# One Fourier filter and expert kernel: loads, small vector steps and one output bank moved in the order of work

## The chip, the cores and the metric

The kernel runs on one core of a Trainium2 chip. The metric is device time in microseconds (us) from launch to end. The engines of the core run side by side, each in the order of its own instruction stream: TensorE (PE, matrix products into PSUM; PEld its weight loads), VectorE (DVE), ScalarE (ACT), GpSimd (POOL, here the indirect scatters) and SyncE (SP, which issues most DMA transfers).

## The reference, cut to what matters

Each of 8 sequences of 2496 rows and 256 columns is filtered in the frequency domain; each filtered row then goes through the one of 8 experts that its gate prefers.

```python
X = np.fft.rfft(x, axis=1)
y = np.fft.irfft(X * (filt_r + 1j * filt_i), n=2496, axis=1)   # 8 x 2496 x 256
x = y.reshape(8 * 2496, 256)
logits = x @ w_gate                                            # 256 x 8
expert_idx = np.argmax(logits, axis=1)
gate_w = softmax(logits)[rows, expert_idx]
for e in range(8):
    h = np.maximum(x[expert_idx == e] @ w1[e], 0)              # 256 x 1024
    out[expert_idx == e] = gate_w * (h @ w2[e])                # 1024 x 256
```

## The kernel before

**Stages.** First the transform: 16 half sequences (8 sequences by 2 halves of the columns) go through a two-step Fourier transform, the filter and the way back. For a group t of four frequencies, `spec1` transposes (pt, copied to z), `spec2` multiplies (px), `filt_` and `join` apply the filter on VectorE (tr, ti, then p), and `spec3` goes back (pi, copied by ScalarE to U). `forward1` and `loadx` bring in the next half sequence. For each finished sequence `route1` to `route6` find expert and place of every row (plw, copied to lw, transposed to pgl, copied by VectorE to gl), and `inv1` to `inv3` finish its rows (pg, gt, py, yt) and scatter them with POOL into the DRAM buffer xs, sorted by expert. In the same stage the experts' weights are read (`w_load`), scaled by powers of two and stored as high and low f16 halves (wscr).

Then the experts: the sorted rows are worked in blocks of 128. There are 7 pairs of blocks ready after sequence 6, 63 pairs after the last sequence, and single blocks at the end. A pair or a single is a unit k. For a unit, `load` (line 1045) fetches the rows xb, 4 buffers; `loadw` (1077) fetches the first-layer weights wa and the second-layer weights wb of its expert, into one of two or four slots, and the transfer is skipped where the slot holds that expert already. Slots reuse the buffers named cm, bm, T and ff, so a weight load may bear these names, and a first-layer load goes to wa, cm or T, a second-layer load to wb, bm or ff. `prep` (1095 to 1104, VectorE) finds a row scale s, `split` scales the block to two f16 halves xs (1109 ScalarE, 1110 VectorE), `turn` (1124) has SP issue a transposing load xs to xt, one for each block of a pair. `layer1` (1146, into ph) has 24 products of 256 columns for two of a pair's four chunks; ScalarE applies the ReLU (hs, 1154) and the cast (hh, 1156), VectorE takes the difference (hl, 1162, `halves`). `layer2` (1177, into po) runs one unit later, in two parts i = 0 and 1 of 12 products each; then VectorE forms the gate factor g (1187), `out_` (1197) scales po with it, and `send` scatters the output.

**What sets the order.** Every step is entered in a list with `at(key, ...)`, the list is sorted by its key (a due time), and the engines' streams are written in that order. No engine passes over a waiting instruction. Keys of the expert stage count from the unit's due time z with its length u: in before, rows are loaded at z - 2.1 u, wa at about z - 1.24 u (or after the last user of the slot), the first block is prepared at z - 1.35 u, split 0.1 and turned 0.15 later.

**Banks.** The outputs po of all blocks share the one bank of the pool pO (tag pO, 1 buffer), the chunks ph the two of pH. The transform's tiles share pF (4 buffers), and plw, pgl and the other routing tiles the single bank of pD.

Of the kernel before, what the change touches and what calls it, by code (L numbers as in the profile page):

```python
# [9 lines left out]
F32 = mybir.dt.float32  # L10
# [5 lines left out]
ALU = mybir.AluOpType  # L16
# [5 lines left out]
S, D, E, F = 2496, 256, 8, 1024  # L22
# [123 lines left out]
def tile_fft_moe(ctx, tc, x, filt_r, filt_i, w_gate, w1, w2, cst, out):  # L146
    nc = tc.nc
    B = x.shape[0]
# [58 lines left out]
    with ExitStack() as fctx:  # L207
# [635 lines left out]
        ps = pD.tile([128, 512], F32, name="pwarm", tag="pD")  # L843
# [31 lines left out]
        def at(key, f, *a):  # L875
            work.append((key, f, a))
# [21 lines left out]
        RT = (0.0, 0.4, 0.65, 1.05, 1.5, 1.75, 2.5, 2.55, 2.9, 3.3)  # L898
        slow = lambda t: min(1.0, max(0.6, 1.0 - 0.06 * (t - 72)))
        for t in range(NT):  # L900
            u, it = divmod(t, 5)
            rho = slow(t)
            at(t, spec1, t)
            w = t + (0.98 if t % 2 == 0 and 3 < t < 72 else 0.0)
# [4 lines left out]
            if u + 1 < NU_ALL and it == 0:  # L909
                for j in range(6):  # L910
                    z = 4.02 + 0.1 * j if u < 1 else t + K["f"] + K["fd"] * j
                    at(z + 1.2 - 0.1 * j if u == 1 else z, forward1, u + 1, j)
            if u % 2 == 0 and it == 0 and u + 2 < NU_ALL:
                for c in range(5):
                    z = t + K["f"] + K["fd"] * (c if c < 4 else 5) + 0.35
# [5 lines left out]
        OPEN = 76.6  # L921
        done = []
        y2 = {}
        for b in range(B):
            rho = slow(10 * b + 9)
            s0 = 10 * b + 9 + K["s3"] * rho + 0.05
            c = 1.0 if b < B - 1 else 0.6
            v = 1.5 if b < B - 2 else c
            y = (0.5, 1.3, 2.1) if b < B - 2 else (0.4 * c, 0.9 * c, 1.2 * c)
            for i, f in enumerate(  # L930
                (
                    (route1, 0),
                    (route1b, 0),
                    (route1, 1),
                    (route1b, 1),
                    (route2,),
                    (route3,),
                    (route4,),
                    (route4b,),
                    (route5,),  # L940
                    (route6,),
                )
            ):
                at(s0 + v * RT[i], f[0], b, *f[1:])
            lead = 3.2 if b < B - 2 else 2.0 if b < B - 1 else 1.3


            t = 10 * b + 20
            d = 0.35
            if b < B - 1:  # L950
                z = PLACE[0] + 0.3 if b == B - 2 else t + K["s3"] * slow(t) - 0.15
                d = min(0.75, (z - s0 - lead) / (NPAIR - 1))
            for j in range(NPAIR):
                z = s0 + lead + (j // 2 * 2 if b < B - 2 else j) * d + 0.001 * j
                at(z, inv1, b, j)
                at(z + y[1], inv2, b, j)
                y2[b, j] = z + y[1]
                z = max(z + y[2], s0 + v * RT[9] + 0.1 + 0.9 * d * j)
                at(z, inv3, b, j)
            if b in [r for r, _, _ in SEG]:  # L960
                for s, part in enumerate(SEG):
                    if part[0] == b:
                        z0 = s0 + v * RT[9] + 0.2
                        for i in range(5):
                            at((96.0 + i) if s == 2 else z0 + (0.1, 0.25)[s] * i, finish, s)
            done.append(z)
# [4 lines left out]
        for q in range(2 * E):  # L971
            e, i = divmod(q, 2)
            z = K["w"] + K["wp"] * q
            at(z - 2.25, w_load, e, i)
            for d, f, *a in (
                (-0.1, w_max, 0),
                (0.1, w_max, 1),
                (0.15, w_turn),
                (2.3, w_scale),
                (2.37, w_hi, 0),  # L980
                (3.7, w_lo, 0),
                (4.37, w_hi, 1),
                (5.6, w_lo, 1),
                (5.7, w_out),
            ):
                at(z + d, f, e, i, *a)
# [5 lines left out]
        wa, wb, mps = [], [], []  # L992
        st = {}
        hid = {}
# [170 lines left out]
        def layer2(b, i):  # L1165
            k, j = home[b]
            m = units[k][2]
            w = wb[slot[k]]
            if i == 0:
                st[b] = (mps[2].tile([128, D], F32, name=f"po{b}", tag="pO"), *st[b][1:])  # L1170
            ps = st[b][0]
            wv = w[:, 0:4096].rearrange("p (i f d) -> p i f d", i=2, d=D)
            for f in range(4 * i, 4 * i + 4):
                c, e = divmod(f, 4 // m)
                o = (e * m + j) * 128
                for n, (q, r) in enumerate(((0, 0), (0, 1), (1, 0))):
                    nc.tensor.matmul(  # L1177
                        ps,
                        lhsT=hid[k, c][q][:, o : o + 128],
                        rhs=wv[:, r, f],  # L1180
                        start=(f == 0 and n == 0),
                        stop=(f == 7 and n == 2),
                    )
            if i:
                g0 = st[b][1]
                g = mps[0].tile([128, 1], F32, name=f"g{b}", tag="g", bufs=3)
                nc.vector.tensor_tensor(g, g0, w[:, 4096:4098].bitcast(F32), op=ALU.mult)
                st[b] = (ps, g, st[b][2])

        def out_(b):  # L1190
            ps, g, t = st.pop(b)
# [45 lines left out]
        for k in range(nu):  # L1237
            s, i, m, b0 = units[k]
            z, d, _ = tau[b0]
            u = d * m  # L1240
            at(max(opened(s), z - (2.1 * u if m > 1 else 2.0), OPEN + 0.1), load, k)
            old = [j for j in range(k) if slot[j] == slot[k]]
            for n in range(2):
                ahead = (
                    12 - 4 * i - 2 * n if s == 2 and i < 2 else 3.3 + 0.3 * k - 0.5 * n if k < 2 else 1.3 - 0.8 * n
                )
                t = when(old[-1], n) + 0.01 if old else 0.0
                at(max(opened(s) + 0.02, t, span(k)[0] - ahead, OPEN + 0.05), loadw, k, n)
            for q in range(m):
                y = max(opened(s) + 0.3, z - (2.1 if b0 < 2 else 1.35 * u if m > 1 else 1.4)) + 0.4 * d * q  # L1250
                at(y, prep, b0 + q)
                at(y + 0.1, split, b0 + q)
                at(y + 0.15, turn, b0 + q)
            z, p = span(k)
            for i in range(2 * m):
                y = z + p * (i // 2 * 0.5 + i % 2 * 0.25 / m) if m > 1 else z + 0.25 * p * i
                at(y, layer1, k, i)
                at(y + 0.2 * p / m, halves, k, i)
            z, p = span(k + 1)
            for q in range(m):  # L1260
                b = b0 + q
                o = p / m
                at(z + o * (q + 0.5), layer2, b, 0)
                at(z + o * (q + 0.75), layer2, b, 1)
                at(z + o * (q + 0.95), out_, b)
                y = z + o * (q + 0.95) + 0.5
                if y < hold + 2.5:
                    kept[b] = len(kept)
                    y = max(y, hold + 0.3 * kept[b])
                at(y, send, b)  # L1270
# [56 lines left out]
```

## Time and profile before

| | us |
|---|---|
| median of three runs | 1317.54 (1315.71 to 1318.96) |
| profiled execution | 1322.67 |
| its span, first to last instruction | 1320.8 |
| TensorE busy | 1295.3 (98%), 12703 products |
| ScalarE busy | 825.7 (63%) |
| VectorE busy | 748.8 (57%) |
| GpSimd busy | 368.2 (28%) |
| transfers, mean | 147 GB/s |

The profile page gives busy shares over the whole span; it is followed by the view of waits (who waited for whom), by rows in order of time, where the idle time ahead of an instruction stands in square brackets with what ended it, and by windows, which give the busy time and the granted clock of TensorE for a stretch (1.00 is 2.4 GHz throughout, 0.50 would be 1.2 GHz). SPq rows are SP issuing a transfer; their time is that of the issue, not of the transfer.

### The profile page before, as it was taken

Reading aid. Unit: us, or ns where it says so; the run is one execution under the profiler, and the core shown is the slowest. Engines: PE = TensorE matmul, PEld = TensorE weight load, DVE = VectorE, ACT = ScalarE, POOL = GpSimd, SP = SyncE. Lnnn points to the kernel's source line nnn. Section 1 sums busy time; section 2 is a strip of 40 time slices with the busy share of each in tenths; the row PEclk is TensorE's granted clock in tenths of the full one; section 3 lists DMA queues with packets and bytes.
Section 4 is the critical chain, followed back from the end, with each engine's and each line's share of the span. In section 5 each row is a group of like instructions: output and inputs, shape, how many; then the busy total and the mean of one; then the engine's idle time right before and its main releaser. Section 6 shows DMA issues by size and latency. Waiting matters only on the chain.

```text
span 1320.8 us, 34604 instructions
## 1 busy us (share of the span) xinstructions
PE 1295.3 (98%) x12703; PEld 1116.5 (85%) x12703; DVE 748.8 (57%) x2408; ACT 825.7 (63%) x1539; POOL 368.2 (28%) x393
## 2 busy tenths in 40 slices
PE   8999999999999999999999999999999999999998
PEld 6887878878876778888888888888888888889997
DVE  2686776867866564555555545555555555544452
ACT  3566767767665676666666656666666666565564
POOL 5005345444345335422111111111211211121121
PEclk9999999999999999999999999999999999999999
DMA  8756656575636435762344342252253256548964
GB/s 216 207 149 224 204 179 224 170 232 166 202 125 190 96 94 141 216 131 74 83 115 105 106 102 77 74 137 77 74 149 78 75 139 153 144 120 231 289 164 141
DMA packets 167072, 193.99 MB, mean 147 GB/s; under 512 B 105341, under 2 KB 141785, under 8 KB 159220
## 3 DMA queue, kind: packets, MB, share of 16 engines
q1 hardware_dynamic: 146308, 147.15, 41.5%
q0 software_dynamic: 20592, 44.60, 10.8%
q8 instruction: 101, 1.65, 0.5%
q14 instruction: 71, 0.58, 0.2%
HBM read 255.61 MB, written 61.56 MB: 240 GB/s over the span
## 4 chain that ended last, share of the span: by engine, by line
PE 85%; DMA 6%; DVE 3%; issue 2%; ACT 2%; SPq 1%; POOL 0%; POOLq 0%; DVEq 0%; ACTq 0%
PE ph L1146 29%; PE po L1177 28%; PE py L696 6%; PE pi L419 5%; PE px L374 5%; PE f L289 5%; PE pg L681 3%; PE pt L356 2%; DMA xt<-xs 2%; PE plw L544 1%; DMA x<-in_x_dram 1%; DMA xb<-xs 1%; DMA ff<-in_filt_r_dram 1%; SPq L274 0%; ACT hs L1154 0%
## 5 line engine op out<-in xcount | busy, mean ns | idle before, releaser
L1162 DVE TENSOR_TENSOR hl<-hs,hh 128x512 f16<-128x512 f32 x322 | 222.0, 690 | 373.3 <-ACT hh L1156 361.2
L180 POOL DMA_INDIRECT out_dram<-ot,t x150 | 146.1, 974 | 632.5 <-ACT ot L1197 618.6
L1177 PEld LDWEIGHTS <-hh 128*128 128x128 f16 x2576 | 251.3, 98 | 34.4 <-issue 5.5
L180 POOL DMA_INDIRECT xs<-yt,dest x176 | 182.2, 1035 | 305.8 <-ACT T L298 80.3
L1154 ACT ACTIVATE hs<-ph 128x512 f32<-128x512 f32 x322 | 191.4, 594 | 80.3 <-PE ph L1146 72.6
L1156 ACT CAST hh<-hs 128x512 f16<-128x512 f32 x322 | 199.0, 618 | 10.3
L1146 PE MATMUL ph<-xt,cm 128*128 128x256 f16 (+1 forms) x1776 | 192.3, 265 | 2.5 <-DMA xt<-xs 1.3
L1146 PE MATMUL ph<-xt,T 128*128 128x256 f16 (+1 forms) x1728 | 188.2, 266 | 3.3 <-DMA xt<-xs 2.7
L1177 PE MATMUL po<-bm,hh 128*128 128x256 f16 x1104 | 184.8, 273 | 0.6 <-ACT ot L1197 0.6
L1146 PEld LDWEIGHTS <-cm 128*128 128x128 f16 x1776 | 163.8, 98 | 21.0 <-issue 3.5
L1177 PE MATMUL po<-ff,hh 128*128 128x256 f16 x1072 | 179.2, 273 | 0.0
L1146 PEld LDWEIGHTS <-T 128*128 128x128 f16 x1728 | 159.7, 98 | 22.0 <-issue 4.5
L1109 ACT ACTIVATE xs<-xb,s 128x256 f16<-128x256 f32 x161 | 81.7, 508 | 126.0 <-DVE s L1099 118.5
L1177 PE MATMUL po<-bm,hl 128*128 128x256 f16 x552 | 150.5, 273 | 0.0
L1177 PE MATMUL po<-ff,hl 128*128 128x256 f16 x536 | 146.1, 273 | 0.0
L1177 PEld LDWEIGHTS <-hl 128*128 128x128 f16 x1288 | 126.1, 98 | 14.6
L1197 ACT ACTIVATE ot<-po,g 128x256 f32<-128x256 f32 x150 | 71.1, 474 | 104.5 <-PE po L1177 81.2
L289 PEld LDWEIGHTS f<-a,x 117*128 117x128 f32 (+1 forms) x704 | 88.6, 195 | 16.5 <-issue 9.8
L289 PE MATMUL f<-a,x 117*128 117x117 f32 (+1 forms) x704 | 98.2, 282 | 1.6 <-issue 1.4
L391 DVE TENSOR_TENSOR tr<-px,ff 128x512 f32<-128x512 f32 x80 | 54.8, 684 | 78.9 <-PE px L374 61.8
L1110 DVE SCALAR_TENSOR_TENSOR xs<-xb,s,xs 128x256 f16<-128x256 f32 x161 | 77.5, 481 | 25.4 <-ACT xs L1109 25.4
L429 ACT COPY U<-pi 128x256 f32<-128x256 f32 (+1 forms) x160 | 55.2, 407 | 54.7 <-PE pi L419 54.7
(183 smaller groups left out, 1736.0 us busy)
## 6 DMA issues: line engine op xcount, KB each, us to landing
bm<-wscr SPq DMA_DIRECT2D x37, 1040.0 KB
cm<-wscr SPq DMA_DIRECT2D x37, 1024.0 KB
ff<-wscr SPq DMA_DIRECT2D x36, 1040.0 KB
T<-wscr SPq DMA_DIRECT2D x36, 1024.0 KB
xb<-xs SPq DMA_DIRECT2D x161, 130.0 KB
wb<-wscr SPq DMA_DIRECT2D x18, 1040.0 KB
wa<-wscr SPq DMA_DIRECT2D x18, 1024.0 KB
wf<-in_moe_w_dram SPq DMA_DIRECT2D x32, 512.0 KB
```

The source lines that it names most:

```text
L180: nc.gpsimd.indirect_dma_start(out=dst, out_offset=bass.IndirectOffsetOnAxis(ap=idx, axis=0), in_=src, in_offset=None, bounds_check=bound, ...
L289: nc.tensor.matmul(ps[:, n : n + m], lhsT=xt.pop((u, g))[:m], rhs=a1[:m, :m], start=True, stop=True,)
L374: nc.tensor.matmul(ps[64 * a : 64 * a + 64, i, j], lhsT=bm[:, 4 * it + 2 * j + i, 64 * a : 64 * a + 64], rhs=z[:, kk], start=True, stop=True,)
L696: nc.tensor.matmul(ps[:GP].rearrange("p g d -> p (g d)"), lhsT=dm, rhs=gt[:GP].rearrange("p g d -> p (g d)"), start=True, stop=True,)
L1109: nc.scalar.activation(xs_[:, 0], xb[:, :D], AF.Copy, scale=sc)
L1110: nc.vector.scalar_tensor_tensor(xs_[:, 1], xb[:, :D], sc, xs_[:, 0], op0=ALU.mult, op1=ALU.subtract)
L1146: nc.tensor.matmul(ps[:, n * f : n * f + n], lhsT=w[:, p : p + 128], rhs=xt[:, r, c, o1 : o1 + n], start=(a == 0), stop=(a == 5),)
L1154: nc.scalar.activation(s, ps, AF.Relu, scale=1.0 / B23)
L1156: nc.scalar.copy(hh, s)
L1162: nc.vector.tensor_tensor(hl, s, hh, op=ALU.subtract)
L1177: nc.tensor.matmul(ps, lhsT=hid[k, c][q][:, o : o + 128], rhs=wv[:, r, f], start=(f == 0 and n == 0), stop=(f == 7 and n == 2),)
L1197: nc.scalar.activation(ot, ps, AF.Copy, scale=g)
```

## The change

Seven edits, all of order but for the last output's bank:

- `w_load` of the first expert weights gets the key 4.85, which is ahead of the small constants (4.9).
- Pairs of the second segment load their rows 2.5 u ahead instead of 2.1 u; unit 1 of the first segment 1.3 earlier than before.
- Split and turn of a pair's blocks come 0.08 and 0.09 (first block) and 0.03 and 0.04 (second block) behind prep, instead of 0.1 and 0.15, in the second segment. So each transposing load is sorted ahead of a weight load that it stood behind. In the first segment, block 0 gets 0.03 and 0.04, block 1 is prepared 0.14 later and split 0.01 behind that, and block 4 is split 0.33 behind its prep.
- In the last sequence the transposes pgl (second entry of the routing, i = 1) come 0.15 earlier.
- The gate factor g is formed at the start of layer two, i = 0, instead of behind its second part.
- For singles the products of layer two are sorted so that all with the high half hh of a part come first, then those with hl.
- The very last block's po goes to a bank of pH.

```diff
@@ -941,7 +941,7 @@
                     (route6,),
                 )
             ):
-                at(s0 + v * RT[i], f[0], b, *f[1:])
+                at(s0 + v * RT[i] - (0.15 if b == B - 1 and i == 1 else 0.0), f[0], b, *f[1:])
             lead = 3.2 if b < B - 2 else 2.0 if b < B - 1 else 1.3
 
 
@@ -971,7 +971,7 @@
         for q in range(2 * E):
             e, i = divmod(q, 2)
             z = K["w"] + K["wp"] * q
-            at(z - 2.25, w_load, e, i)
+            at(4.85 if q < 1 else z - 2.25, w_load, e, i)
             for d, f, *a in (
                 (-0.1, w_max, 0),
                 (0.1, w_max, 1),
@@ -1167,25 +1167,31 @@
             m = units[k][2]
             w = wb[slot[k]]
             if i == 0:
-                st[b] = (mps[2].tile([128, D], F32, name=f"po{b}", tag="pO"), *st[b][1:])
+                if b == NB - 1:
+                    ps = mps[1].tile([128, 512], F32, name=f"po{b}", tag="pH")[:, :D]
+                else:
+                    ps = mps[2].tile([128, D], F32, name=f"po{b}", tag="pO")
+                g = mps[0].tile([128, 1], F32, name=f"g{b}", tag="g", bufs=3)
+                nc.vector.tensor_tensor(g, st[b][1], w[:, 4096:4098].bitcast(F32), op=ALU.mult)
+                st[b] = (ps, g, st[b][2])
             ps = st[b][0]
             wv = w[:, 0:4096].rearrange("p (i f d) -> p i f d", i=2, d=D)
+            terms = []
             for f in range(4 * i, 4 * i + 4):
                 c, e = divmod(f, 4 // m)
                 o = (e * m + j) * 128
                 for n, (q, r) in enumerate(((0, 0), (0, 1), (1, 0))):
-                    nc.tensor.matmul(
-                        ps,
-                        lhsT=hid[k, c][q][:, o : o + 128],
-                        rhs=wv[:, r, f],
-                        start=(f == 0 and n == 0),
-                        stop=(f == 7 and n == 2),
-                    )
-            if i:
-                g0 = st[b][1]
-                g = mps[0].tile([128, 1], F32, name=f"g{b}", tag="g", bufs=3)
-                nc.vector.tensor_tensor(g, g0, w[:, 4096:4098].bitcast(F32), op=ALU.mult)
-                st[b] = (ps, g, st[b][2])
+                    terms.append((q, r, f, c, o, f == 0 and n == 0))
+            if m == 1:
+                terms.sort(key=lambda v: v[0])
+            for q, r, f, c, o, new in terms:
+                nc.tensor.matmul(
+                    ps,
+                    lhsT=hid[k, c][q][:, o : o + 128],
+                    rhs=wv[:, r, f],
+                    start=new,
+                    stop=(f == 7 and q == 1),
+                )
 
         def out_(b):
             ps, g, t = st.pop(b)
@@ -1238,7 +1244,8 @@
             s, i, m, b0 = units[k]
             z, d, _ = tau[b0]
             u = d * m
-            at(max(opened(s), z - (2.1 * u if m > 1 else 2.0), OPEN + 0.1), load, k)
+            y = z - ((2.5 if s else 2.1) * u if m > 1 else 2.0)
+            at(max(opened(s), y - 1.3 if k == 1 else y, OPEN + 0.1), load, k)
             old = [j for j in range(k) if slot[j] == slot[k]]
             for n in range(2):
                 ahead = (
@@ -1248,9 +1255,14 @@
                 at(max(opened(s) + 0.02, t, span(k)[0] - ahead, OPEN + 0.05), loadw, k, n)
             for q in range(m):
                 y = max(opened(s) + 0.3, z - (2.1 if b0 < 2 else 1.35 * u if m > 1 else 1.4)) + 0.4 * d * q
+                v, w = (0.1, 0.15) if s == 0 or m == 1 else ((0.08, 0.09), (0.03, 0.04))[q]
+                if k == 0:
+                    y, v, w = (y, 0.03, 0.04) if q == 0 else (y + 0.14, 0.01, 0.02)
+                if b0 + q == 4:
+                    v, w = 0.33, 0.34
                 at(y, prep, b0 + q)
-                at(y + 0.1, split, b0 + q)
-                at(y + 0.15, turn, b0 + q)
+                at(y + v, split, b0 + q)
+                at(y + w, turn, b0 + q)
             z, p = span(k)
             for i in range(2 * m):
                 y = z + p * (i // 2 * 0.5 + i % 2 * 0.25 / m) if m > 1 else z + 0.25 * p * i
```

What this does to SP's order, in the middle of the pairs (unit 20; xt20 is written by the transposing loads of blocks 40 and 41; T1 is here a first-layer weight load, ff2 and bm second-layer ones; rows that look up the table and set registers are left out). Before:

```order
L1124 DMA_TRANSPOSE xt19_9754<-xs39_9762 128x4x128
L1077 DMA T1_108<-wscr_58 128x4096
L1124 DMA_TRANSPOSE xt20_9942<-xs40_9917 128x4x128
L1045 DMA xb42_9980<-xs_57 128x260
L1045 DMA xb43_9982<-xs_57 128x260
L1077 DMA bm_106<-wscr_58 128x4160
L1124 DMA_TRANSPOSE xt20_9942<-xs41_9950 128x4x128
L1077 DMA cm_105<-wscr_58 128x4096
L1124 DMA_TRANSPOSE xt21_10130<-xs42_10105 128x4x128
```

After:

```order
L1124 DMA_TRANSPOSE xt19_9748<-xs39_9777 128x4x128
L1077 DMA ff2_124<-wscr_58 128x4160
L1045 DMA xb42_9901<-xs_57 128x260
L1045 DMA xb43_9903<-xs_57 128x260
L1124 DMA_TRANSPOSE xt20_9941<-xs40_9930 128x4x128
L1077 DMA T1_108<-wscr_58 128x4096
L1124 DMA_TRANSPOSE xt20_9941<-xs41_9965 128x4x128
L1077 DMA bm_106<-wscr_58 128x4160
```

The second transposing load of unit 20 stood behind the rows of unit 21 and the second-layer weights bm; now it stands right behind the first-layer weights T1 and ahead of bm, and the first one has gone ahead of T1. The rows of unit 21 are ahead of both.

ScalarE at the handover (xs0 and xs1 are the scaling of expert blocks 0 and 1; U3, z78, gt and yt are copies of the transform). Before:

```order
L708 COPY yt6_2_5828<-py6_4_5826 117x2x256
L429 COPY U3_121<-pi75_0_5843 128x64x3
L429 COPY U3_121<-pi75_1_5844 128x64x4
L362 COPY z78_5869<-pt78_5864 128x512
L1109 ACTIVATE xs0_5836<-xb0_5789,s0_5832 128x256
L687 COPY gt6_6_5878<-pg6_6_5873 117x512
L1109 ACTIVATE xs1_5899<-xb1_5791,s1_5895 128x256
```

After:

```order
L708 COPY yt6_2_5832<-py6_4_5830 117x2x256
L1109 ACTIVATE xs0_5840<-xb0_5789,s0_5836 128x256
L429 COPY U3_121<-pi75_0_5851 128x64x3
L429 COPY U3_121<-pi75_1_5852 128x64x4
L362 COPY z78_5877<-pt78_5872 128x512
L687 COPY gt6_6_5884<-pg6_6_5879 117x512
L1109 ACTIVATE xs1_5914<-xb1_5791,s1_5910 128x256
```

The scaling of block 0 has moved ahead of two U copies and of z78. On VectorE, in the same place, the two instructions that make p77 now stand ahead of the prep of block 1. On TensorE the transposes pgl of the last sequence stand ahead of the first chunk of unit 1 instead of behind it.

## Rows read from the trace of the kernel before

**Rows 1.** Waits of TensorE, whole span: total us, times, longest us.

```profile
PE ph L1146 <- DMA xt<-xs: 4.0, 4, 2.1
PE ph L1146 <- issue: 1.7, 3, 1.0
PE po L1177 <- ACT ot L1197: 1.5, 3, 0.6
```

**Rows 2.** TensorE in order of time: start us, us, instruction [idle before, ended by].

```profile
57.33 3.69 PE L419 MATMUL pi<-cm,p 64*128 64x128 f32 x32 [2.40 <-DVE p L400]
...
424.05 1.16 PE L419 MATMUL pi<-cm,p 64*128 64x128 f32 x14 [0.72 <-DVE ti L391]
425.76 1.65 PE L374 MATMUL px<-z,bm 128*64 128x128 f32 x16 [0.56 <-ACT yt L708]
427.35 2.06 PE L696 MATMUL py<-gt,dm 117*117 117x512 f32 x2
...
430.25 1.02 PE L696 MATMUL py<-gt,dm 117*117 117x512 f32 x2
...
445.38 0.80 PE L544 MATMUL plw<-U,wg 128*32 128x351 f32 x8 [0.76 <-ACT U L429]
...
450.91 1.39 PE L544 MATMUL plw<-U,wg 128*32 128x351 f32 x16 [0.73 <-DVE yt L715]
...
528.42 2.78 PE L1146 MATMUL ph<-xt,cm 128*128 128x256 f16 x24 [0.68 <-DMA xt<-xs]
...
773.15 4.21 PE L1146 MATMUL ph<-xt,T 128*128 128x256 f16 x24 [2.11 <-DMA xt<-xs]
...
1312.92 0.38 PE L1177 MATMUL po<-wb,hh 128*128 128x256 f16 x2 [0.56 <-ACT ot L1197]
```

**Rows 3.** Windows, TensorE alone: stretch, length, busy us, granted clock, DMA share, GB/s.

```profile
425.00:430.00 5.00, 4.44 (x26) 0.66 0.98 253
...
775.00:780.00 5.00, 5.00 (x36) 0.73 0.35 94
```

**Rows 4.** ScalarE and VectorE at the handover, in order of time.

```profile
418.51 0.59 ACT L708 COPY yt<-py 117x512 f32<-117x512 f32 x1 [0.22 <-PE py L696]
...
421.69 0.51 ACT L1109 ACTIVATE xs<-xb,s 128x256 f16<-128x256 f32 x1
...
422.24 0.48 DVE L1110 SCALAR_TENSOR_TENSOR xs<-xb,s,xs 128x256 f16<-128x256 f32 x1 [4.05 <-ACT xs L1109]
...
424.73 0.51 ACT L1109 ACTIVATE xs<-xb,s 128x256 f16<-128x256 f32 x1 [2.05 <-DVE s L1099]
...
444.66 0.67 ACT L429 COPY U<-pi 128x256 f32<-128x256 f32 x2
...
450.61 0.16 DVE L574 COPY gl<-pgl 117x8 f32<-117x8 f32 x1
```

**Rows 5.** SP issuing, among the pairs, in order of time.

```profile
557.60 0.35 SPq L1077 DMA_DIRECT2D cm<-wscr  x1
...
760.69 1.20 SPq L1124 DMA_TRANSPOSE xt<-xs  x1
...
764.57 0.33 SPq L1077 DMA_DIRECT2D bm<-wscr  x1
765.00 1.22 SPq L1124 DMA_TRANSPOSE xt<-xs  x1
...
1152.33 0.34 SPq L1077 DMA_DIRECT2D cm<-wscr  x1
```

**Rows 6.** Chain that ended last, in order of time: start us, us, what.

```profile
765.00 8.01 DMA xt<-xs
...
885.20 5.58 DMA xt<-xs
```

**Rows 7.** TensorE and VectorE near 53 us, in order of time.

```profile
52.95 1.97 PE L374 MATMUL px<-z,bm 128*64 128x128 f32 x32
...
54.46 0.68 DVE L391 TENSOR_TENSOR tr<-px,ff 128x512 f32<-128x512 f32 x1
```

## The prediction

> **What bounds the kernel now.** I began with TensorE, because the page calls it busy for nearly the whole span, and asked where it still waits: the view of waits says for whom, TensorE's rows in order of time say where [rows 1, 2]. Outside the fill at the start there are four places. At the handover from the transform to the experts (about 424 to 451 us) it stands idle four times, 0.72, 0.56, 0.76 and 0.73 us. Among the pairs of blocks (528 to 1103 us) the first layer waits seven times, 4.0 us under the name of the transposing load and 1.7 us under no name, 5.7 us together. The output bank is waited for three times, 1.5 us, the last time 0.56 us at the very end. The fourth is one 2.40 us wait for the product p near 57 us. The granted clock belongs to it [rows 3]: after the two waits at 424 it is 0.66 in 425 to 430, after the 2.11 us wait at 771 it is 0.73 in 775 to 780, so part of these stretches ran at 1.2 instead of 2.4 GHz. Rows of the same work at either level give the price: py takes 2.06 instead of 1.02 us, 24 matmuls of ph take 4.21 instead of 2.78 us [rows 2].
>
> **Part 1, the handover.** ScalarE finishes a yt copy at 419.10 and scales block 0 only at 421.69, behind two U copies and a z; VectorE stands 4.05 us for it, and then comes ti, which TensorE's pi waits for [rows 2, 4]. The block's scale was set by VectorE before that copy ended, so with xs0 right behind the copy it fits at 419.1 to 419.6, into ScalarE's own pause. VectorE then does xs0 by 420.1, tr and ti of group 77 by 421.9, and the 0.72 us wait at 424.05 goes. Next late is the yt copy behind ScalarE's xs1, which ran at 424.73 for 0.51 us [rows 4]. In the new order VectorE does p77 first (0.8 us more ahead of it) and yet is 2.1 us earlier, so xs1 ends near 423.8, the copy near 424.4, and px starts then instead of at 425.76, with TensorE free at about 423.9: some 0.45 us of the 0.56 stays. So 0.83 us of idle time goes. One wait of 0.45 us leaves the clock alone, if the waits of 0.76, 0.73 and 0.68 us are the measure, behind which the matmuls keep their full rate [rows 2]; then py gains 1.04 us, px, which took 1.65 us, some more. Busy 4.44 us at 0.66 of the clock is 4.44 x 0.34 = 1.5 us, and I take that.
>
> Later, the second half of plw waits 0.76 us for U copies that stand behind the scaling of block 4 [rows 2, 4]. That scaling takes about 0.5 us; with it behind the copies they end near 444.8 and 0.2 us is left, so 0.56 us goes. The transposes pgl stand half a first-layer chunk earlier, and VectorE's copies of them before a difference hl: they ended at about 450.8 [rows 4], and the next plw, waiting for their bank, started at 450.91. They can now be done near 448.3, before TensorE asks at about 449.5, and 0.73 us goes. Sum of part 1: 0.83 + 1.5 + 0.56 + 0.73 = 3.6 us; from below 2.1 (the clock falls all the same), from above 4.3 (the 0.45 goes too, and px's share of the clock is more).
>
> **Part 2, loads among the pairs.** SP issues in order. In before the second transposing load of a pair stands right behind the second-layer weights of the pair ahead. Most weight issues are skipped (the expert is the same); where one is real it takes 0.33 us to issue, as at 764.57, and the transposing load behind it, issued at 765.00, takes 8.01 us; at 885.20 it is 5.58 us [rows 5, 6]. TensorE was due at 773.15 - 2.11 = 771.04. In the new order that load stands ahead of these weights: first transposing load at 760.69 for 1.20 us, a weight issue of up to 0.35, then the second at about 762.3. Behind a skipped weight issue nothing is ahead of it. So six of the waits go, and the one at 528.42 (0.68 us) goes as the rows of the next pair no longer stand between its two transposing loads, which brings the second 1 us forward: 5.7 us. The clock behind 773.15 gives 4.21 - 2.78 = 1.4 us more. Sum 7.1 us; from below nearly nothing, if the recorded execution alone has these waits.
>
> What is queued behind moves too. The weights of the second layer wait on SP for TensorE until 764.57 and the second transposing load is out 2 us before, so they are not held; the rows 2.5 pairs ahead need a buffer of four whose block was split long before. The first-layer weights now wait behind the first transposing load, so they are issued at about 762.0 instead of up to 4 us earlier, 9 us before use.
>
> On that order, the Trainium skill has a rule (DMA: Bandwidth & Descriptors, Queues, rings and completion order): each DMA engine takes one issuing engine's descriptors in ring order. The 8.01 us of [rows 6] agree. By it nothing is won where the load ahead is real; the same page's Bandwidth table has 6.15 us for 1 MB, and with that, as an estimate, weights issued at 762.0 are in by 768.2, before TensorE is due.
>
> **Part 3, singles and the end.** With the gate factor ahead of layer two VectorE forms it before the next split (0.5 us) rather than behind it, and ScalarE's output copy leaves earlier: of the three waits for the output bank one of about 0.4 us goes. The last output in a bank of its own, whose earlier user ScalarE emptied some 3 us before, takes the 0.56 us at 1312.92 off the chain that ends the kernel. The third, where the pairs end, stays. 1.5 - 0.56 = 0.9 us. Sorting the terms of layer two by half changes no count; TensorE shows no wait for hl there, so 0. The factor formed earlier waits for second-layer weights that TensorE needs at the same moment: 0.
>
> **Part 4, the start.** The first expert weights are issued about 5 us earlier, ahead of the small constants, so VectorE's reductions of them end before px is there. But px is ready, half of 1.97 us after 52.95, at 53.9, and tr starts at 54.46 [rows 7]; six VectorE instructions stand between px and pi either way. So only 0.5 us of the 2.40 goes, from 0 to 2.4. The constants land later, with room.
>
> **Sum against the recorded execution**: 3.6 + 7.1 + 0.9 + 0.5 = 12.1 us from 1322.67. That execution is 5.1 us above the median of 1317.54. Its 8.01 us transfer is the odd one beside 5.58: were it like the others, the wait would be some 0.6 us, and 1.5 + 1.4 = 2.9 us of the gain would be the recorded execution's own. I take them out: 12.1 - 2.9 = 9.2, so 1317.5 - 9.2 = **1308**.
>
> **The rivals.**
> A, slower than before: the wait changes place. The second transposing load now stands behind real first-layer weights, seven times between 557.60 and 1152.33 [rows 5]. It has from 762.3 to 771.04, 8.7 us. For: 8.01 us behind an equal load is close. Against: 5.58. Each us beyond 8.7 costs seven waits, and the clock with them, 1.4 us for 2.11, so 7 x 1.7 = 12 us. From a landing time of 9.5 us on the gain is gone, at 9.8 the kernel is 0.3% slower, about 1321. This is the ring-order mechanism of part 2.
> B, the pair waits and the clock drop belong to the recorded execution: what stays is 0.83 + 0.56 + 0.73 + 0.9 + 0.5 = 3.5 us, 1314. For: it is 5.1 us above the median. Against: seven waits in one execution, six of them behind a real load, are a rule of the order, not an accident.
> C, the handover's gain turns into a wait: TensorE reaches the first layer at 431.6 instead of 433.95 and finds its transposing load late, or the clock falls on the 0.45 us that stays. Part 1's first half (2.3 us) goes: 1308 + 2.3 = 1310. Against: the load is issued earlier as well.
> D, all of the 12.1 us shows in the median: 1305.5.
> E, the change doesn't do what it says: the second split comes later than the second-layer weights could go, and the order only exchanges who waits: 1317. Against: about 2 us between the two in the rows.
>
> **How the numbers follow.** Forecast 1308 (own range 1306 to 1310) 0.42; D 0.20; C 0.14; B 0.12; E 0.07; A 0.05. The range 1303 to 1314 takes in D with more of the start, the forecast, C and B, and leaves out A, E and little else. This kernel's times tell 0.3% apart, 4 us, so faster means below 1313.6: forecast, D, C and nearly half of B, 0.81. Within: the rest of B, E, 0.13. Slower: A and a little, 0.06.
>
> **What would show it.** In the profile after: no wait of ph for xt at second-layer loads, and none at the seven real first-layer loads (A would stand there); VectorE's 4.05 us before xs0 gone and granted clock 1.00 in the stretch of px and py; one wait of about 0.4 us before px; no wait before the last po; still about 2 us before pi near 57 us. I am wrong if the waits stay, or if the waits go and the time doesn't follow.

## The result, and the profile after

The changed kernel takes 1306.09 us (median of six runs, 1305.6 to 1311.78), the kernel before beside it 1319.1 (six runs, 1315.71 to 1321.61): a ratio of 0.9912, 95% interval 0.9891 to 0.9933. It is 13.0 us faster; the prediction said 1308 in a range of 1303 to 1314. The profiled execution of after took 1306.08 us, its span is 1304.3.

TensorE's waits in after (total us, times, longest us), the rows that answer to [rows 1]:

```profile
PE po L1188 <- ACT ot L1203: 1.8, 2, 1.2
PE px L374 <- ACT yt L708: 0.5, 1, 0.5
PE ph L1146 <- DMA xt<-xs: 0.3, 1, 0.3
```

The first layer waits 0.3 us where it waited 5.7. TensorE in order of time, to be laid beside [rows 2]:

```profile
55.23 2.10 PE L419 MATMUL pi<-cm,p 64*128 64x128 f32 x32
...
420.79 1.09 PE L374 MATMUL px<-z,bm 128*64 128x128 f32 x16 [0.49 <-ACT yt L708]
421.81 1.12 PE L696 MATMUL py<-gt,dm 117*117 117x512 f32 x2
...
519.96 2.78 PE L1146 MATMUL ph<-xt,cm 128*128 128x256 f16 x24 [0.27 <-DMA xt<-xs]
...
1186.77 0.38 PE L1188 MATMUL po<-bm,hh 128*128 128x256 f16 x2 [0.56 <-ACT ot L1203]
...
1235.85 1.03 PE L1188 MATMUL po<-wb,hh 128*128 128x256 f16 x8 [1.22 <-ACT ot L1203]
```

Behind 40 us these are TensorE's only waits of a quarter of a microsecond and more, save 0.51 at 51.86 and 0.49 at 68.80, which before has too (51.48, 72.50). The 2.40 us near 57 are gone, of the four handover waits one of 0.49 is left, the pairs have none behind the 0.27 us at their first one (519.96), and the last output has none. The granted clock in the two stretches of [rows 3] (length, busy us, clock, share of the transfer engines, GB/s):

```profile
425.00:430.00 5.00, 5.00 (x53) 1.00 0.54 147
775.00:780.00 5.00, 5.00 (x49) 1.00 0.49 125
```

**Where the 13 us come from.** Three places of TensorE's stream are easily found in every profile: the transposes pt behind a 0.15 us wait near 370 us, the first pair's ph at 528.42 [rows 2], and the output bank's 0.56 us wait where the pairs end. In before the first and the last are

```profile
369.97 0.63 PE L356 MATMUL pt<-ident,T 128*128 128x128 f32 x4 [0.15 <-DVE ti L391]
...
1202.92 0.38 PE L1177 MATMUL po<-bm,hh 128*128 128x256 f16 x2 [0.56 <-ACT ot L1197]
```

They cut the span into start, handover, pairs and end. The table has one profiled execution of each kernel; the kernels other than the two are those of the experiments below.

| kernel | start | handover | pairs | end |
|---|---|---|---|---|
| before | 369.97 | 158.45 | 674.50 | 117.9 |
| start alone | 365.31 | 157.82 | 675.42 | 118.6 |
| pairs alone (rows and turns) | 367.75 | 156.44 | 666.98 | 118.2 |
| handover alone | 371.61 | 155.84 | 669.77 | 118.3 |
| layer two alone | 368.46 | 157.87 | 671.88 | 117.5 |
| after | 366.27 | 153.69 | 666.81 | 117.5 |
| after, singles' rows earlier | 367.19 | 153.34 | 667.12 | 116.1 |
| after, first-layer loads all real | 365.45 | 153.44 | 668.79 | 116.8 |
| rows alone, second-layer loads all real | 367.11 | 157.05 | 671.03 | 118.4 |
| turns alone, second-layer loads all real | 367.10 | 156.49 | 682.11 | 116.8 |

Executions of kernels with the same order differ by up to 6 us in a column, so I take means over the kernels that share an order. Start: six with the old order 368.7, four with the new 366.1, so 2.6 us. Handover: 158.0 (before, start alone, layer two alone) against 153.5 (the three forms of after), 4.5 us. Pairs: 672.9 (the four with the old order) against 667.0 (pairs alone, after, singles' rows earlier), 5.9 us. End: 118.2 (before, start alone, pairs alone, handover alone) against 117.5 (layer two alone, after), 0.7 us, though turns alone has 116.8 with the old end, so this difference is no larger than the scatter. The sum is 13.7 us, where the medians give 13.0.

### The profile page after: what moved, and what is told of

Same layout as the page of the kernel before. It is cut to its first block, busy times and chain, and to the rows that moved or that the text cites. A ratio compares the mean times of both kernels' runs of the same rounds, so it can differ in the third digit from the quotient of the medians.

```text
span 1304.3 us, 34542 instructions
## 1 busy us (share of the span) xinstructions
PE 1288.8 (99%) x12703; PEld 1113.6 (85%) x12703; DVE 749.0 (57%) x2408; ACT 821.4 (63%) x1539; POOL 369.1 (28%) x393
## 4 chain that ended last, share of the span: by engine, by line
PE 57%; issue 30%; POOL 7%; DVE 3%; DMA 2%; ACT 1%; SPq 1%; POOLq 1%; DVEq 0%; ACTq 0%
PE ph L1146 14%; PE po L1188 14%; POOL out_dram L180 7%; PE py L696 6%; PE pi L419 5%; PE f L289 5%; PE px L374 5%; PE pg L681 3%; PE pt L356 2%; PE plw L544 1%; DMA bm<-c_bm_dram 1%; DMA x<-in_x_dram 1%; SPq L274 0%; PE pgl L562 0%; ACT U L429 0%
## 5 line engine op out<-in xcount | busy, mean ns | idle before, releaser
L1188 PE MATMUL po<-bm,hh 128*128 128x256 f16 x1104 | 181.6, 273 | 0.6 <-ACT ot L1203 0.6
L1188 PE MATMUL po<-ff,hh 128*128 128x256 f16 x1072 | 176.2, 273 | 0.0
L1188 PE MATMUL po<-bm,hl 128*128 128x256 f16 x552 | 145.5, 273 | 0.0
L1188 PE MATMUL po<-ff,hl 128*128 128x256 f16 x536 | 141.2, 273 | 0.0
```

The lines of the kernel that those rows point to most:

```text
L1188: nc.tensor.matmul(ps, lhsT=hid[k, c][q][:, o : o + 128], rhs=wv[:, r, f], start=new, stop=(f == 7 and q == 1),)
```

## The experiments

### Each part alone

Four kernels, each the kernel before with one part of the change, ran beside it on one chip (before: 1320.02 us).

The first expert weights ahead of the small constants:

```diff
-            at(z - 2.25, w_load, e, i)
+            at(4.85 if q < 1 else z - 2.25, w_load, e, i)
```

> The kernel before with one edit: the first expert weights are issued ahead of the small constants. Theory S (VectorE's reductions of these weights stood ahead of the filter product that needs only the earlier px, so all of the 2.40 us wait near 57 us and the low clock behind it go): no wait of TensorE for p near 57 us, granted clock 1.00 in 55 to 60 us, plw at 72.5 us some 3.5 to 4 us earlier, 1315.4 us where the kernel before has 1319.1. Rival, as predicted: about 1.9 us of the wait stays and the time falls by 0.5 us, 1318.6. Second rival: the gain is lost again at the handover, where the DMA rows and not TensorE set the time: 1319.

Measured: 1317.69 us, ratio 0.9979 (0.9959 to 0.9999), 2.3 us. The wait for p near 57 us is gone, and the place behind it, plw at 72.50 us in before, comes at 67.83. So the step gives more than the 0.5 us that I gave it. This rests on the profile: the interval of the times, 0.1 to 5.4 us, does not exclude 0.5.

The pairs, rows and turns together:

```diff
-            at(max(opened(s), z - (2.1 * u if m > 1 else 2.0), OPEN + 0.1), load, k)
+            at(max(opened(s), z - ((2.5 if s else 2.1) * u if m > 1 else 2.0), OPEN + 0.1), load, k)
...
+                v, w = (0.1, 0.15) if s == 0 or m == 1 else ((0.08, 0.09), (0.03, 0.04))[q]
-                at(y + 0.1, split, b0 + q)
-                at(y + 0.15, turn, b0 + q)
+                at(y + v, split, b0 + q)
+                at(y + w, turn, b0 + q)
```

> The kernel before with the second segment's loads alone: rows 2.5 pairs ahead, split and turn sorted ahead of the weight loads. Theory P (the second transposing load waited in SP's ring behind real second-layer weights): no wait of ph for xt between 530 and 1103 us, no low clock behind one, time lower by 7 to 8 us, 1311.5 against 1319.1. Rival B (the waits belong to the recorded execution): profile as in theory P, time lower by 1 us at most, 1318. Rival A (the wait goes to the pairs with real first-layer weights): about seven waits of 1 to 2 us remain, 1317 to 1321.

Measured: 1311.16 us, ratio 0.9931 (0.9911 to 0.9951), 8.9 us with an interval of some 6.5 to 12. Its profile has no wait of ph for xt at all; pairs and handover are 5.9 and 1.6 us shorter than the means with the old order.

The handover (pgl 0.15 earlier, unit 1's rows 1.3 earlier, split and turn of blocks 0, 1 and 4), the same lines as in the diff of the change:

> The kernel before with the handover's order alone: rows of blocks 2 and 3 ahead of unit 1's weights, block 0 scaled ahead of the U copies, block 4 behind them, pgl earlier. Theory H (VectorE's wait for the scaling of block 0 held the filter product and the banks behind it): VectorE's 4.05 us before xs0 down to about 1.3, TensorE's waits at 424, 445 and 451 us gone, that at 426 down to 0.5, granted clock 1.00 in 425 to 430 us, 3.5 to 4.5 us less, 1315 against 1319.1. Rival C (the gain becomes a wait for the transposing load of the first pair, or for the rows at 515 us): TensorE's waits go, a new one of 2 to 4 us stands at the first layer or near 528 us, time within 1 us of before.

Measured: 1316.52 us, ratio 0.9968 (0.9948 to 0.9988), 3.5 us. All four handover waits go but for one of 0.49 us. But the first pair finds its transposing load late:

```profile
527.45 2.78 PE L1146 MATMUL ph<-xt,cm 128*128 128x256 f16 x24 [2.05 <-DMA xt<-xs]
```

That is rival C's mechanism, mostly at the pairs' first load (unit 0's is 0.32 us late at 433.07): TensorE comes earlier, the load does not. With the pairs' part beside it, in after, 0.27 us of it is left.

Layer two (gate factor ahead, sorted terms for singles, last output in its own bank), the diff's lines from `if b == NB - 1` on:

> The kernel before with layer two alone changed: gate factor formed ahead of it, products of singles sorted by half, last output in its own bank. Theory L: only the 0.56 us wait of the last po goes, 0.5 to 1.0 us less, 1318.4, not to be told from no change by the time, and to be read in the profile alone. Rival: the gate factor's earlier place stops VectorE on second-layer weights that are not there yet; then new waits of VectorE for these weights and 1 to 5 us more.

Measured: 1320.7 us, ratio 1.0001 (0.9977 to 1.0025). The last wait of 0.56 us is gone in its profile, the other two waits for the output bank are not; 0.7 us can't be seen in the times.

The four parts together are 2.3 + 8.9 + 3.5 - 0.7 = 14.0 us, the whole 13.0: the parts add, as far as intervals of 2 to 3 us either way for each of them can tell.

### What makes the second transposing load late

My prediction said: it stands behind the second-layer weights. The part has two edits, so each was run alone. These two and the next two kernels ran on another chip, where before itself takes 1393.69 us; I use their profiles of the pairs, which run at the same pace there.

> The kernel before with the rows of the second segment's pairs 2.5 pairs ahead and nothing else; the second transposing load still stands behind the second-layer weights. Theory P (it is the place behind these weights that costs): the waits of ph for xt at real second-layer loads stay, 2 to 8 us in the profile as in the kernels that keep the old order, only the wait near 528 us shrinks, time within 2 us of before, 1318 to 1320. Rival R (the rows standing between the two transposing loads cost): the waits go, 1311.

Measured: 1390.61 us, ratio 0.9982 (0.9949 to 1.0015). Pairs 669.0 us, no wait of ph.

> The kernel before with split and turn of the second segment's pairs sorted ahead of the weight loads and nothing else; the rows stay 2.1 pairs ahead. Theory P: no wait of ph for xt between 530 and 1180 us, 1311 to 1313 as with both edits. Rival R: the waits stay, 1319.

Measured: 1393.31 us, ratio 0.9996 (0.9963 to 1.0029). Pairs 672.4 us; no wait of ph for xt, but four of po, 0.23 to 0.95 us, three of them named after second-layer weights. The times leave both open. So the suspected cause was made larger: in before, and in after, every second-layer load of the 63 pairs is really made, also where the slot holds the expert (the output stays the same).

```diff
+            if units[k][0] == 1 and i == 1:
+                nc.sync.dma_start(
+                    (wa, wb)[i][slot[k]],
+                    wscr[bass.ds(ex, 1), :, o : o + n].rearrange("o p f -> p (o f)"),
+                )
+                return
```

> The kernel before, where each of the 63 pairs of the second segment loads its second-layer weights, whether the slot holds them or not (some 55 loads of 1.04 MB more; the output is the same). Theory P: nearly every pair then waits for its second transposing load, 0.3 to 2 us each, 20 to 110 us in all, 1340 to 1430 us. Rival B (the waits are accidents of an execution, not of the place behind real weights): a few us of waits as before, 1320 to 1325.

> The kernel after with the same 63 second-layer loads all made. Theory P: the transposing load stands ahead of these weights, so no wait of ph for xt, 1306 to 1312 us. Rival D (the transfers themselves are too many, and whatever is behind them comes late): waits at every pair as in the kernel before with the same loads, 1340 or more.

Measured, one run each: 1431.11 us for the old order, 37 above before, and 1383.13 for the new, 11 below before. Pairs 708.3 and 670.4 us. TensorE's waits, the old order:

```profile
PE ph L1152 <- DMA xt<-xs: 20.2, 17, 3.3
PE ph L1152 <- issue: 10.0, 14, 1.7
```

and the new:

```profile
PE ph L1152 <- issue: 1.3, 2, 1.1
```

The two of the new order stand at 576 to 578 us, ahead of the 63 pairs, which begin at 593; in the pairs it has none, where the old order has 29. So a real load there is what turns the old order into waits, and the new order bears it. Position behind the weights explained this, as my step had it. The last pair of kernels tests it: the amplified kernel with the rows moved and the position kept, and with the turns moved and the rows kept (back on a usual chip, before 1320.37 us).

> The kernel before with every second-layer weight load of the pairs' segment really made (the load that is skipped where the slot holds the expert is made too; the output stays the same), and of the change only the rows' loads 2.5 pairs ahead. Theory P (position: what makes TensorE wait is that the second transposing load of a pair stands behind a real second-layer load on SP's queue): the load still stands there, so the waits of ph stay as in the amplified kernel before, some 30 us in all (20.2 named after the transposing load, 10.0 after nothing), and the time is 30 to 40 us above the kernel before on this chip. Theory R (rows: the waits come from the next pair's rows standing between the two transposing loads, and these have now moved): waits under 8 us, time within 10 us of the kernel before. In the unamplified pair of runs neither part could be told from no change.

Measured: 1315.39 us, 5 below before (one run). Waits of ph 2.8 us in four pairs, not 30 us in 29. SP (time of issue, us) and the ph that it serves:

```profile
747.38 1.23 SPq L1130 DMA_TRANSPOSE xt<-xs  x1
749.02 0.35 SPq L1078 DMA_DIRECT2D ff<-wscr  x1
749.47 1.47 SPq L1130 DMA_TRANSPOSE xt<-xs  x1
...
752.14 0.92 SPq L1045 DMA_DIRECT2D xb<-xs  x2
...
757.57 2.78 PE L1152 MATMUL ph<-xt,cm 128*128 128x256 f16 x24
```

> The same amplified kernel before, and of the change only the keys of split and turn among the pairs (transposing loads sorted ahead of the weight loads; the rows stay 2.1 pairs ahead, as before). Theory P: waits of ph under 5 us, time at or up to 6 us below the kernel before. Theory R: the rows still stand in between, waits of 15 to 30 us, time 15 to 37 us above the kernel before. If both of these two kernels keep part of the waits, both parts are needed.

Measured: 1324.34 us, 4 above before (one run), pairs 682.1 us. No wait of ph, but others in its place:

```profile
PE po L1183 <- ACT ot L1203: 4.2, 5, 2.0
PE po L1183 <- DMA bm<-wscr: 3.8, 6, 1.3
PE po L1183 <- DMA ff<-wscr: 3.8, 5, 1.7
```

and SP there:

```profile
763.08 1.24 SPq L1130 DMA_TRANSPOSE xt<-xs  x1
764.82 0.09 SPq L1083 DMA_DIRECT2D T<-wscr  x1
765.02 1.19 SPq L1130 DMA_TRANSPOSE xt<-xs  x1
...
767.48 0.92 SPq L1045 DMA_DIRECT2D xb<-xs  x2
768.81 0.33 SPq L1078 DMA_DIRECT2D bm<-wscr  x1
...
772.56 2.78 PE L1152 MATMUL ph<-xt,T 128*128 128x256 f16 x24
...
775.18 0.38 PE L1183 MATMUL po<-bm,hh 128*128 128x256 f16 x2
```

The position theory falls. In the kernel with the rows moved the second transposing load stands directly behind a real 1 MB load at every pair, and TensorE hardly waits for it. With a real load ahead, what counts is the lead: how long before TensorE's ph the load is issued. In before it was issued at 765.00 for 771.04, a lead of 6.0 us [rows 2, 5]. Between the end of the first load's issue, 761.89, and the weights at 764.57 lay the rows with the look-ups, 2.7 us of SP's time; with the rows out of the way this step is 0.4 us (748.61 to 749.02) and the lead 757.57 - 749.47 = 8.1 us. A landing time of 5.58 to 8.01 us [rows 6] is covered by 8.1, and by 6.0 only at its shortest. It can be longer: the longest wait left in the kernel with the rows moved, 1.08 us at 684.14, follows a load issued at 674.81, 9.3 us before. In the amplified old order, in a pair where ph was due at 804.52 - 1.45 = 803.07, the lead is 4.8 us:

```profile
796.35 1.84 SPq L1078 DMA_DIRECT2D ff<-wscr  x1
...
798.28 1.43 SPq L1130 DMA_TRANSPOSE xt<-xs  x1
...
804.52 2.78 PE L1152 MATMUL ph<-xt,cm 128*128 128x256 f16 x24 [1.45 <-DMA xt<-xs]
```

Whatever stands behind the rows is late. With the turns alone the transposing load stands ahead of them, its lead is 772.56 - 765.02 = 7.5 us, and ph does not wait; but now it is the weights, issued at 768.81 for 775.18, 6.4 us ahead, where in the kernel with the rows alone ff is issued at 749.02 and wanted at 760.18, 11.2 us. That is rival E's exchange of who waits, in half of the change. Either edit takes the waits of ph away; the rows' edit does it without putting others in their place, so it carries the part, while the turns alone leave the pairs 11 us longer with real loads (682.1 against 671.0). That the amplified old order and the last two kernels ran on different chips is a weakness of this comparison. Before itself, on a usual chip, bears it out on a small scale: seven of its pairs have a real second-layer load right ahead of their second transposing load, with leads of 5.1 to 6.1 us, and six of them wait.

### Rival A, and the wait that is left

After with every first-layer load of the 63 pairs real, the same edit with `i == 0`:

> The changed kernel with every first-layer weight load of the pairs' segment really made; the output stays the same. The second transposing load of a pair now stands behind a real load of 1 MB at every pair instead of seven times. Rival A of the prediction: the transposing load lands 8 us and more behind its issue, some 8.7 us before it is needed, so waits of ph of 0.5 us and more appear at many of the 63 pairs, 30 us or more in all, as they do in the kernel before with real second-layer loads. The forecast's side (it is early enough): waits of ph under 3 us in all, and a time within 6 us of what the changed kernel has beside the kernel before, thus some 10 to 15 us below the kernel before on this chip.

Measured: 1306.26 us (one run), 14 below before. Two waits of ph, 1.0 us together, one of them at the end of this transfer (the chain that ended last: start us, us, what; then TensorE):

```profile
532.81 8.38 DMA xt<-xs
```

```profile
541.33 2.78 PE L1152 MATMUL ph<-xt,cm 128*128 128x256 f16 x24 [0.66 <-DMA xt<-xs]
...
1097.82 2.78 PE L1152 MATMUL ph<-xt,T 128*128 128x256 f16 x24 [0.37 <-DMA xt<-xs]
```

Rival A set the lead at 8.7 us and the end of the gain at a landing time of 9.5. The lead was over-sized: at the seven real first-layer loads of after it is 8.0 us at six and 7.3 at one, because the second transposing load is issued 2.2 us behind the first (740.91 and 743.09) and not 1.6. By the rival's own price the gain would end near 8.8. None of the seven pairs waits, and with all the loads real one pair in thirty does: 8.38 us where 7.9 were to be had, and at 1097.82 a start 8.7 us behind the load's issue where 8.3 were to be had. The Trainium skill (DMA: Bandwidth & Descriptors, Queues, rings and completion order) says that each DMA engine takes the descriptors of a ring in order. These runs agree, as far as a transposing load behind a real 1 MB load takes up to 8.38 us here; they show too that a lead of about 8 us pays for it nearly always.

The 1.22 us wait at 1235.85 in after: VectorE stands for a single block's rows, ahead of the gate factor that ScalarE's output copy needs.

```profile
1228.66 0.34 SPq L1077 DMA_DIRECT2D wb<-wscr  x1
...
1230.17 0.34 SPq L1045 DMA_DIRECT2D xb<-xs  x1
...
1233.46 0.42 DVE L1095 TENSOR_REDUCE m<-xb 128x1 f32<-128x257 f32 x1 [3.46 <-DMA xb<-xs]
...
1235.09 0.15 DVE L1175 TENSOR_TENSOR g<-g,bm 128x1 f32<-128x1 f32 x1
...
1235.33 0.47 ACT L1203 ACTIVATE ot<-po,g 128x256 f32<-128x256 f32 x1 [0.53 <-DVE g L1175]
```

So the singles' rows were moved ahead of that weight load:

```diff
-            y = z - ((2.5 if s else 2.1) * u if m > 1 else 2.0)
+            y = z - ((2.5 if s else 2.1) * u if m > 1 else 2.6)
```

> The changed kernel with the rows of the single blocks loaded 2.6 instead of 2.0 ahead of their due time, so that they are issued ahead of a weight load that they stood behind. Theory S (the wait for the output bank that is left at 1235.85 us, 1.22 us, comes from VectorE standing 3.46 us for a single's rows, behind 1 MB weight loads, so that gate factor and output are late): VectorE's waits for rows among the singles, 5.7 us in three in the changed kernel, go, the 1.22 us wait of TensorE goes with them, and the time is about 1 us below the changed kernel, ratio to the kernel before some 0.990. Rival G (the wait is the output copy's own, and ScalarE is late whatever VectorE does): the waits of TensorE among the singles stay at 1.2 to 1.8 us, time as that of the changed kernel, ratio 0.991. Rival W (the rows moved ahead make the weights behind them late): a wait of TensorE for weights, 1 us or more.

Measured: 1309.45 us (1304.7 to 1310.62), ratio 0.9918 (0.9899 to 0.9938). VectorE's waits for rows are gone and the 1.22 us wait with them; TensorE's rows for the output bank are now

```profile
PE po L1188 <- ACT ot L1203: 1.0, 2, 0.6
```

and the end is 116.1 us instead of 117.5. This fits theory S, but 1.4 us is not seen in the times: 0.9918 and 0.9912 are the same. It is one profile each, and the wait varies: in the kernel with real first-layer loads, whose singles have the order of after, it is 0.38 us. So the mechanism is likely, not shown.

## Why the prediction was right, point by point

It was right to 2 us, with two terms too small and one reason wrong. That it came so near is in part luck: the gain was forecast as 9.2 us and measured as 13.0, and before, the base that it was taken from, ran 1319.1 us beside after and not 1317.5, which took back 1.6 of the 3.8.

**Start: the mis-sized step.** Forecast 0.5 us, measured 2.6 by the means and 2.3 by the times. I read [rows 7] as if tr at 54.46 waited for the px of 52.95. The rows leave out buffer numbers: tr's own px is the row of that name before, at 44.75, done 8 us earlier. Here are px, the two reductions of the weights and tr; of before:

```profile
44.75 1.97 PE L374 MATMUL px<-z,bm 128*64 128x128 f32 x32
...
50.68 1.22 DVE L455 TENSOR_REDUCE wm<-wf 128x1 f32<-128x1024 f32 x1 [8.14 <-DMA wf<-in_moe_w_dram]
...
52.69 1.22 DVE L455 TENSOR_REDUCE wm<-wf 128x1 f32<-128x1024 f32 x1 [0.57 <-DMA wf<-in_moe_w_dram]
```

and of after:

```profile
47.03 1.22 DVE L455 TENSOR_REDUCE wm<-wf 128x1 f32<-128x1024 f32 x1 [3.65 <-DMA wf<-in_moe_w_dram]
...
50.52 1.22 DVE L455 TENSOR_REDUCE wm<-wf 128x1 f32<-128x1024 f32 x1
...
52.30 0.68 DVE L391 TENSOR_TENSOR tr<-px,ff 128x512 f32<-128x512 f32 x1
...
53.33 1.97 PE L374 MATMUL px<-z,bm 128*64 128x128 f32 x32
```

In after tr starts a microsecond ahead of the px that I took it to wait for. What held VectorE in before was the weights' load, 8.14 us, so the earlier load takes away the whole wait, 2.40 us in before's recorded execution and 1.4 to 2.3 in five others with the old order. The upper bound that the step gave, 2.4, was near the answer. The step also left out the clock: pi behind the 2.40 us took 3.69 us [rows 2], at a granted clock of 0.57 in 57 to 61 us, where it takes 2.10 in after. Not every execution pays this: in pairs alone pi takes 2.17 us behind a wait of 2.22.

**Handover.** Forecast 2.1 us without the clock, and 0.7 at 528.42; measured 4.5 by the means. The steps went as told: xs0 follows the yt copy (415.28 after 414.80), VectorE's wait for it is 1.34 us instead of 4.05, the 0.72, 0.76 and 0.73 us waits go, one of 0.49 stays before px where 0.45 was told, and the clock is 1.00:

```profile
414.80 0.58 ACT L708 COPY yt<-py 117x512 f32<-117x512 f32 x1 [0.22 <-PE py L696]
415.28 0.51 ACT L1109 ACTIVATE xs<-xb,s 128x256 f16<-128x256 f32 x1
...
415.83 0.48 DVE L1110 SCALAR_TENSOR_TENSOR xs<-xb,s,xs 128x256 f16<-128x256 f32 x1 [1.34 <-ACT xs L1109]
```

Taking the clock's 1.5 us out as the recorded execution's own was right, though the reason given, one long transfer among the pairs, has nothing to do with the handover: with the same waits of 0.73 and 0.56 us, start alone has a clock of 1.00 in 422 to 428 us, and so have pairs alone and layer two alone. But each of these has a wait that before's recorded execution did not show, pg for ti, 0.71, 0.23 and 0.49 us, and in before's place at 528.42 they (save pairs alone) have 0.94 and 1.22 us instead of 0.68. The sum was too small because one execution's list of waits is not the list.

```profile
433.11 0.67 PE L681 MATMUL pg<-ident,U 128*117 128x128 f32 x4 [0.71 <-DVE ti L391]
```

**Pairs.** Forecast 5.0 us (5.7 less the 0.7 at 528.42, without the clock), measured 5.9: right in size, and wrong in its reason for six of the seven waits. The failed step is "in before the second transposing load stands right behind the second-layer weights"; that is so, and nearly harmless with a lead of 8 us. The lead was 6 because the next pair's rows stood between the two, the reason that the prediction gave for the wait at 528.42 alone. The price of the rows on SP was in [rows 5], in the step from 760.69 to 764.57, which the prediction took for a wait of the weights for TensorE. The view of SP's waits in before, 530 to 1150 us (total us, times, longest us), has for second-layer weights only

```profile
SPq L1077 <- PE po L1177: 0.3, 1, 0.3
```

The 1.4 us that were taken out for the clock behind 773.15 were the recorded execution's own: behind a wait of 2.05 us the same 24 products take 2.78 us in handover alone.

**Singles and end.** Forecast 0.9, measured 0.7 by the means, within the scatter. The 0.56 us at the end went. The other wait did not: the gate factor was late because VectorE stood for rows, ahead of it in either order. In after that wait is 1.22 us.

**The rivals.** A fell: after has no wait at the seven real first-layer loads, though its lead is 8.0 us and not 8.7. B fell: without amplified loads, the kernels with the old order have 1.8 to 6.8 us of waits of ph between 530 and 1150 us in their profiles, those with the pairs' part none. C shows in the handover alone and is taken away by the pairs' part. D's time, 1305.5, is nearer than the forecast's, but its reason, that the clock's share shows, is not what happened: the start's 2.1 us more and the handover's stand where the 2.9 us were. E holds for the turns alone, not for the change.

## What to carry to other kernels

For a transfer that comes late in a queue, subtract its time of issue from the time at which it is wanted, and look at what fills the issuing engine's time just ahead of it: here two small loads with their look-ups cost 2.1 us of lead, and the 1 MB load that looked guilty did little harm once they were gone. Move what is wanted last to the back, and look who then stands behind it. Before saying that an instruction waits for a row, see which of the rows of that name it reads: where buffer numbers are left out, it can be an earlier one.

## What the runs showed of the hardware

The drop of the granted clock behind short waits is not a fixed price: with the same two waits of 0.7 and 0.56 us it was 0.66 behind them in before's execution and 1.00 in those of start alone, pairs alone, layer two alone and the kernel with the rows alone and real second-layer loads.

One chip ran the kernel before in 1393.69 us, where others take 1320. The pairs keep their pace there, 669 to 672 us without amplified loads. The difference lies in the transform: there TensorE stands again and again for nothing that the profile shows, in the midst of runs of equal products. Windows from 100 to 500 us (busy us of TensorE, of its weight loads, VectorE, ScalarE and GpSimd; clock, share of the transfer engines, GB/s), of after on the one chip and of after with real second-layer loads on the other, ahead of the pairs that have these loads:

```profile
100.00:500.00 400.00, 398.63 (x3963) 315.56 (x3962) 275.32 (x770) 273.14 (x529) 175.05 (x175) 1.00 0.56 172
```

```profile
100.00:500.00 400.00, 367.37 (x3451) 283.81 (x3449) 240.61 (x620) 229.82 (x452) 148.07 (x150) 0.95 0.52 160
```

```profile
118.26 0.51 PE L419 MATMUL pi<-cm,p 64*128 64x128 f32 x4 [1.03 <-issue]
```

What holds it up is not shown by any run here.
